# Later stores of x: nine places for the attention output, and the first expert's weights one period later

## The chip, the cores and the metric

The kernel runs on one core of a Trainium2 chip. The metric is device microseconds from the start to the end of one execution, and less is better. The core has TensorE (PE; its weight loads are listed as PEld), VectorE (DVE), ScalarE (ACT), GpSimd (POOL) and SyncE (SP), which here only issues DMAs; 16 DMA engines move the data.

## The reference, cut to what matters

Chunked attention (each head in chunks of 64 tokens, softmax inside a chunk) makes x, and a mixture of experts with one expert per token works on x. Which expert a token goes to depends on the logits of x, and, where the local gate says so, on the token before it.

```python
B, H, S, D = q.shape            # 8, 8, 576, 64
scores = scale * np.matmul(q_c, k_c.transpose(0, 1, 2, 4, 3))   # chunks of 64
attn = np.exp(scores - np.max(scores, axis=-1, keepdims=True))
attn = attn / (np.sum(attn, axis=-1, keepdims=True) + 1e-09)
x = np.matmul(attn, v_c) ...    # then (8, 576, 512)

logits = np.einsum('bsd,de->bse', x, w_gate)                    # 8 experts
local_gate = 1.0 / (1.0 + np.exp(-np.einsum('bsd,de->bse', x, w_local).squeeze(-1)))
...
        for s in range(S):
            fresh_e = int(np.argmax(logits[b, s]))
            if s == 0 or local_gate[b, s] < 0.5:
                e = fresh_e
            else:
                e = prev_e if prev_e >= 0 else fresh_e
            prev_e = e
            ls = logits[b, s] - logits[b, s].max()
            p = np.exp(ls)
            p /= p.sum() + 1e-09
            h = np.maximum(x[b, s] @ w1[e], 0.0)                # w1: 512 x 1024 each
            out[b, s] = p[e] * (h @ w2[e])                      # w2: 1024 x 512 each
```

## The kernel before

The 4608 tokens are 18 tiles of 256, numbered 0 to 17. The attention runs as a pipeline of periods written out by hand: period i makes the scores of tile i+1 (`sc`), transposes of its probabilities later on, the values of tile i-1 (`o`, then x by the divide of line 267 into `xs`), the transposes and the router logits of tile i-2 (`xs` read, its last columns filled by line 316), the transposes of q and k of tile i+2, and on GpSimd the copies that pair the heads of tile i+3. Periods 1 to 15 are a loop; what comes before and after is written as two long lists, "start" and "drain".

In a period TensorE's order is: scores, transposes of `xs`, the first half of the values, transposes of q, router, transposes of k, the second half of the values, router transposes, transposes of the probabilities. The two halves share one tile of PSUM, `o`, so that the second half waits until VectorE has written the first into `xs`.

Loads and stores of this part are issued by SyncE, in the order that the framework settles on; at most eight of its DMAs are under way, since each waits for the one eight before it. In period i they are q and k of tile i+5 (three buffers each), v of tile i+2 (three buffers, the third of them in the memory of the raw half of w2 until tile 12, then two), and the store of x of tile i-2 to `x_d` in DRAM (line 318), right after its logits are there. x has three places (`xs`, three buffers), so tile i's x goes to the place of tile i-3 and its first write waits for the landing of that store. The first expert's w1 (four quarters, `raw1`) is loaded at the ends of periods 9 to 12, its w2 at the ends of 13 and 14, and w1 is split into a high part (ScalarE, line 102) and a low part (GpSimd, line 103) at the ends of periods 11 to 14.

```python
xss[i] = pa2.tile([P, 2, XR], F32, name="xs", bufs=3)              # a_va, the values of tile i
...
nc.sync.dma_start(x_d[256 * i:256 * i + 256, :].rearrange("(c p) n -> p c n", p=P), xs)   # red, line 318
...
        if 9 <= i < 13:                                            # end of period i
            load_w1(0, i - 9)
        if i in (13, 14):
            for c in range(2 * i - 26, 2 * i - 24):
                load_w2(0, c)
        if 11 <= i < 15:
            for col in (slice(0, 512), slice(512, F)):
                split(w1h[i - 11][:, col], w1l[i - 11][:, col], raw1[i - 11][:, col], nc.gpsimd)
```

After the periods the tokens are sorted by expert, gathered in tiles of 128 from `x_d` by indirect DMAs on GpSimd, and put through w1 (line 646) and w2 (line 660). Three tiles of the first expert are gathered early, from the first 2304 tokens (tiles 0 to 8), so that their matmuls fill the drain. The experts take the time from about 166 us to the end.

Of the kernel before, what the change touches and what calls it, by code (L numbers as in the profile page):

```python
# [8 lines left out]
F32 = mybir.dt.float32  # L9
F32R = mybir.dt.float32r  # L10
# [12 lines left out]
C = H * D  # L23
N = B * S
P = 128
NT = N // P
NS = N // 256
XR = C + E + 1
# [30 lines left out]
    "t1": "AAAA",  # L59
    "t2": "AVAA",  # L60
    "steady": "lq s*8 s h0 tx*8 s va*4 va tq*8 ra*2 h1 tq*8 pr*4 va*4 lv va ra*2 h2 tp*8 s h3 ",
    "hooks": [47, 47, 49, 49, 51, 51, 53, 54, 55, 55, 57, 58, 58, 59, 59, 61, 62, 62],
}

# [2 lines left out]
def tile_attention_then_moe(ctx: ExitStack, tc, q, k_in, v, wg, wl, w1, w2, out):  # L67
    nc = tc.nc

    cpool = ctx.enter_context(tc.tile_pool(name="cpool", bufs=1))  # L70
    wpool = ctx.enter_context(tc.tile_pool(name="wpool", bufs=1))
    dpool = ctx.enter_context(tc.tile_pool(name="dpool", bufs=1, space=DRAM))

    x_d = dpool.tile([N, XR], F32, name="x_d")
# [10 lines left out]

    w1h = [wpool.tile([P, F], F32R, name=f"w1h{c}") for c in range(4)]
    w1l = [wpool.tile([P, F], F32R, name=f"w1l{c}") for c in range(4)]
    w2h = [wpool.tile([P, 2, C], F32R, name=f"w2h{c}") for c in range(4)]
    w2l = [wpool.tile([P, 2, C], F32R, name=f"w2l{c}") for c in range(4)]
    pair1 = [wpool.tile([P, 2, F], F32, name=f"raw1_{g}") for g in range(2)]  # L90
    pair2 = [wpool.tile([P, 4, C], F32, name=f"raw2_{g}") for g in range(2)]
    raw1 = [pair1[c // 2][:, c % 2] for c in range(4)]
    raw2 = [pair2[c // 2][:, c % 2 * 2:c % 2 * 2 + 2] for c in range(4)]

    def load_w1(e, c):
        nc.sync.dma_start(raw1[c], w1[e, P * c:P * c + P, :])
# [4 lines left out]
    def split(hi, lo, raw, lo_eng=None):  # L101
        nc.scalar.copy(hi, raw)  # L102
        (lo_eng or nc.vector).tensor_tensor(lo, raw, hi.bitcast(F32), ALU.subtract)  # L103
# [5 lines left out]
    pa2 = ctx.enter_context(tc.tile_pool(name="pa2", bufs=2, side="right"))  # L109
# [8 lines left out]
    vbuf = [pa1.tile([P, 2, H, DV], F32, name=f"v{i}") for i in range(2)]  # L118
    vbuf.append(pair2[1].rearrange("p a c -> p (a c)")[:, 0:2 * H * DV].rearrange("p (c h d) -> p c h d", c=2, h=H))
    V3 = 12  # L120

    def cut(i):
        n = -256 * i % S
# [166 lines left out]
    def router(i, xT, xs, fine=False):  # L290
        lg = ps_l.tile([P, 2, 256], F32, name="lg")
        lT = pa2.tile([P, 2, 256], F32, name="lT", bufs=1)

        def mm():
            for c in range(4):
                nc.tensor.matmul(lg[32 * c:32 * c + 32, 0], wg9[:, c], xT[:, c], start=True, stop=True)  # L296
            if not fine:
                cp()

        def cp():  # L300
            nc.vector.tensor_copy(lT[:, 0], lg[:, 0])
            nc.vector.tensor_copy(lT[:, 1].rearrange("p (c a q) -> p a c q", a=2, c=2),
                                  lg[:, 0].rearrange("p (a c q) -> p a c q", a=2, c=2))

        def tr():
            for cc in range(2):
                nc.tensor.transpose(lg[:, 1, P * cc:P * cc + P], lT[:, 0, P * cc:P * cc + P], ident)
            for cc in range(2):
                nc.tensor.transpose(lg[:, 0, P * cc:P * cc + P], lT[:, 1, P * cc:P * cc + P], ident)
            if not fine:  # L310
                red()

        def red():
            Lt = L[:, 2 * i:2 * i + 2, :]
            for n, dst in ((0, xs[:, :, C:XR]), (1, Lt)):
                nc.vector.tensor_reduce(
                    dst, lg[:, n].rearrange("p (t c e) -> p t e c", t=2, c=4)[:, :, 0:9, :], AX.X, ALU.add)
            nc.sync.dma_start(x_d[256 * i:256 * i + 256, :].rearrange("(c p) n -> p c n", p=P), xs)

        return [mm, cp, tr, red] if fine else [mm, tr]  # L320

    def ok(i):
        return 0 <= i < NS
# [123 lines left out]
    qk, hd, vts, qkT, prs, pTs, xss, xTs = ({} for _ in range(8))  # L447
# [15 lines left out]
        return p_transposes(prs.pop(i), pTs[i], fine)  # L463

    def a_va(i, fine=False):
        xss[i] = pa2.tile([P, 2, XR], F32, name="xs", bufs=3)
        return values(pTs.pop(i), vts.pop(i), xss[i], fine)

    def a_tx(i, fine=False):
# [359 lines left out]
    for i in range(1, NS - 2):  # L829
        qs4 = dict(s=lambda: a_sa(i + 1), tp=lambda: a_tp(i), va=lambda: a_va(i - 1, True), tq=lambda: a_tq(i + 2))  # L830
        opt = dict(lq=load(qk, load_qk, i + 5) if ok(i + 5) else None,
                   lv=(lambda: [lambda: load_vs(i)]),
                   pr=(lambda: a_pair(i + 3)) if ok(i + 3) else None, tx=(lambda: a_tx(i - 2)) if i >= 2 else None, ra=(lambda: a_ra(i - 2, True)) if i >= 2 else None)
        for h in range(4):
            opt[f"h{h}"] = (lambda h=h: [lambda: run(hooks[i, h])]) if (i, h) in hooks else None
        toks = [t for t in PAR["steady"].split() if opt.get(t.split("*")[0], 1) is not None]
        play(" ".join(toks), qs4 | {k: v for k, v in opt.items() if v is not None})
        if 9 <= i < 13:
            load_w1(0, i - 9)
        if i in (13, 14):  # L840
            for c in range(2 * i - 26, 2 * i - 24):
                load_w2(0, c)
        if 11 <= i < 15:
            for col in (slice(0, 512), slice(512, F)):
                split(w1h[i - 11][:, col], w1l[i - 11][:, col], raw1[i - 11][:, col], nc.gpsimd)

    def w2_split(c):
        return [lambda: nc.scalar.copy(w2h[c], raw2[c]),
# [4 lines left out]
    n = NS - 1  # L853
# [265 lines left out]
```

## Time and profile before

| what | value |
|---|---|
| time, median of 3 runs | 673.91 us (673.85 to 678.2) |
| the profiled execution: time, span | 675.2 us, 673.4 us |
| PE, DVE, ACT, POOL busy | 633.6, 362.6, 267.5, 150.8 us |
| bytes moved | 98.23 MB, mean 146 GB/s |
| share of 16 DMA engines in the first nine slices of 16.8 us | 0.9 and more in each |

The span is the time from the first to the last instruction in the profile. Rows of stretches give, after the bounds and the length, the busy time and the count of instructions of PE, PEld, DVE, ACT and POOL, then TensorE's granted clock (1.00 is its full level of 2.4 GHz, 0.50 the lower one of 1.2 GHz), the busy share of the DMA engines (packets that overlap can take it above 1) and GB/s. In rows of waits and of timelines the arrow points to what ended the wait. A line of scores, `sc`, is the first work of a period on TensorE: period 4 begins at 47.07 us, period 13 at 122.06 us.

### The profile page before, as it was taken

The page shows a single profiled execution, that of the slowest core. Times are in us where ns is not written, and L with a number is a line of the kernel's source. Part 1 is how long each engine was busy: PE and PEld are TensorE (multiplying, and loading weights), DVE is VectorE, ACT ScalarE, POOL GpSimd, SP SyncE. Part 2 cuts the span into 40 slices and gives each one's busy share as a digit, 9 for nine tenths or more (in the row PEclk, how much of TensorE's full clock was granted, in tenths as well). Part 3 has the DMA queues.
Part 4 walks back from the last instruction along what each step waited for, and adds up shares of the span by engine and source line. Part 5 has one row for each costly group of instructions (what it writes and reads, how often), then busy time and mean ns, then how long its engine had stood idle before and what let it go on. Part 6 is the DMA issues. An engine that isn't in the chain of part 4 may idle for free.

```text
span 673.4 us, 16385 instructions
## 1 busy us (share of the span) xinstructions
PE 633.6 (94%) x5684; PEld 503.2 (75%) x5684; DVE 362.6 (54%) x936; ACT 267.5 (40%) x439; POOL 150.8 (22%) x214
## 2 busy tenths in 40 slices
PE   5899989888999999999999999999999999999993
PEld 4677777666777887778888877788877888768872
DVE  2656667686787376663232466643467422564230
ACT  4657667656322235442122343422454222442220
POOL 5323224472022111211121121221122211212101
PEclk9989999998999999999999999999999999999998
DMA  9999999995614114545111153551148511244101
GB/s 230 249 229 258 236 264 280 301 282 164 236 37 143 33 49 174 177 160 177 35 64 34 33 191 145 191 172 44 38 171 292 176 38 34 66 158 167 48 19 37
DMA packets 102829, 98.23 MB, mean 146 GB/s; under 512 B 42388, under 2 KB 79252, under 8 KB 102676
## 3 DMA queue, kind: packets, MB, share of 16 engines
q1 hardware_dynamic: 88644, 61.01, 32.7%
q0 software_dynamic: 6640, 20.65, 9.2%
q10 hardware_dynamic: 7392, 14.68, 6.2%
q8 instruction: 77, 1.26, 0.8%
q14 instruction: 76, 0.62, 0.3%
HBM read 77.28 MB, written 20.35 MB: 145 GB/s over the span
## 4 chain that ended last, share of the span: by engine, by line
PE 39%; issue 26%; DMA 23%; DVE 5%; SPq 3%; POOL 2%; POOLq 1%; ACT 0%; DVEq 0%
DMA out<-ysb,sidx 14%; PE y L660 12%; PE h L646 12%; DMA x_d<-xs 7%; PE tr L174 4%; SPq L135 3%; PE o L253 2%; PE tr L740 2%; DVE xs L267 2%; PE tr L725 1%; PE y L667 1%; POOL rh L441 1%; DMA qt<-in_q 1%; PE h L654 1%; PE lg L296 1%
## 5 line engine op out<-in xcount | busy, mean ns | idle before, releaser
L660 PE MATMUL y<-w2h,hp 128*128 128x512 f32 x560 | 185.8, 401 | 1.0 <-ACTq L954 1.0
L646 PE MATMUL h<-w1h,xp 128*128 128x512 f32 x560 | 161.6, 398 | 0.0
L775 POOL DMA_INDIRECT out<-ysb,sidx x41 | 41.9, 1021 | 369.9 <-DVE ysb L772 284.3
L660 PEld LDWEIGHTS y<-w2h,hp 128*128 128x128 f32 x560 | 105.2, 188 | 24.8 <-ACTq L954 1.2
L646 PEld LDWEIGHTS h<-w1h,xp 128*128 128x128 f32 x560 | 102.1, 188 | 20.1 <-issue 0.2
L660 PE MATMUL y<-w2l,hp 128*128 128x512 f32 x280 | 110.7, 395 | 0.1
L646 PE MATMUL h<-w1l,xp 128*128 128x512 f32 x280 | 87.3, 393 | 0.4 <-DVEq L954 0.4
L713 ACT CAST hp<-tr 128x512 fp32r<-128x512 f32 x64 | 34.9, 589 | 119.5 <-PE tr L740 116.8
L772 DVE TENSOR_SCALAR ysb<-y,ppr 128x512 f32<-128x512 f32 x35 | 26.3, 750 | 87.4 <-PE y L660 68.1
L646 PEld LDWEIGHTS h<-w1l,xp 128*128 128x128 f32 x280 | 52.5, 188 | 12.4 <-DVEq L954 0.9
L660 PEld LDWEIGHTS y<-w2l,hp 128*128 128x128 f32 x280 | 52.7, 188 | 11.5 <-DVEq L954 0.6
L699 ACT ACTIVATE hsb<-h 128x1024 f32<-128x1024 f32 x35 | 35.9, 1026 | 60.2 <-PE h L646 57.6
L714 DVE TENSOR_TENSOR xp<-tr,xp 128x512 fp32r<-128x512 f32 x32 | 22.1, 690 | 58.9 <-ACTq L954 56.2
L714 DVE TENSOR_TENSOR hp<-tr,hp 128x512 fp32r<-128x512 f32 x64 | 41.6, 685 | 15.5 <-ACT hp L713 13.7
L632 ACT ACTIVATE pex<-pex 128x8 f32<-128x8 f32 x41 | 8.6, 209 | 102.4 <-DVE pex L631 89.1
L613 POOL DMA_INDIRECT xg<-x_d,gidx x39 | 41.4, 1063 | 14.1 <-issue 10.1
L740 PEld LDWEIGHTS tr<-ident,hsb 128*128 128x128 f32 x274 | 31.9, 140 | 9.0 <-ACTq L954 3.3
L740 PE MATMUL tr<-ident,hsb 128*128 128x128 f32 x274 | 37.3, 274 | 1.4 <-DVEq L954 1.4
L103 DVE TENSOR_TENSOR w1l<-raw,w1h 128x1024 fp32r<-128x1024 f32 x28 | 33.0, 1222 | 8.3 <-ACT w1h L102 8.3
L103 DVE TENSOR_TENSOR w2l<-raw,w2h 128x1024 fp32r<-128x1024 f32 x28 | 32.4, 1220 | 3.9 <-ACT w2h L102 3.9
L166 POOL COPY qr<-qt 128x512 f32<-128x512 f32 x34 | 19.9, 613 | 65.3 <-PE tr L174 44.0
L267 DVE TENSOR_TENSOR xs<-o,rs 128x512 f32<-128x512 f32 x36 | 24.9, 693 | 14.5 <-DMA x_d<-xs 13.6
(210 smaller groups left out, 851.5 us busy)
## 6 DMA issues: line engine op xcount, KB each, us to landing
raw<-in_moe_w SPq DMA_DIRECT2D x14, 1024.0 KB
raw<-in_moe_w ACTq DMA_DIRECT2D x14, 1024.0 KB, 6.4
x_d<-xs SPq DMA_DIRECT2D x18, 521.0 KB, 6.0
raw<-in_moe_w SPq DMA_DIRECT2D x16, 512.0 KB
v<-in_v SPq DMA_DIRECT2D x26, 256.0 KB, 7.0
qt<-in_q SPq DMA_DIRECT2D x11, 512.0 KB, 6.5
kt<-in_k SPq DMA_DIRECT2D x11, 512.0 KB, 7.6
qt<-in_q SPq DMA_DIRECT2D x16, 128.0 KB, 3.8
```

Of the source, the lines that this page charges most:

```text
L103: (lo_eng or nc.vector).tensor_tensor(lo, raw, hi.bitcast(F32), ALU.subtract)
L174: nc.tensor.transpose(box["ps"][:, n], src_of(n), ident)
L267: nc.vector.tensor_tensor(xs[:, :, 256 * j:256 * j + 256].rearrange("p c (h d) -> p c h d", d=D), ov[:, :, :, 0:D], rs.unsqueeze(3).to_bro ...
L613: nc.gpsimd.indirect_dma_start(out=dst, out_offset=None, in_=src, in_offset=bass.IndirectOffsetOnAxis(ap=gidx[t].bitcast(U32), axis=0))
L646: nc.tensor.matmul(hs[:, j], xs[a][:, c], W1[w][c][:, 512 * j:512 * j + 512], start=(c == 0 and n == 0), stop=(c == 3 and n == 2))
L660: nc.tensor.matmul(y, hx[f // 4][a][:, f % 4], W2[w][c][:, f % 2, :], start=(f == 0 and n == 0), stop=(f == 7 and n == 2))
L699: nc.scalar.activation(hsb, hs.rearrange("p j f -> p (j f)"), AF.Relu)
L713: nc.scalar.copy(p[:, 0], ps)
L714: V.tensor_tensor(p[:, 1], ps, p[:, 0].bitcast(F32), ALU.subtract)
L740: nc.tensor.transpose(ps[:, n], hsb[:, at + P * n:at + P * n + P], ident)
L772: either(kind and kind[1], lambda: V.tensor_scalar(ysb, y, pr, None, ALU.mult), lambda: y_part(ysb, y, pr))
L775: nc.gpsimd.indirect_dma_start(out=out, out_offset=bass.IndirectOffsetOnAxis(ap=sidx[t].bitcast(U32), axis=0), in_=ysb, in_offset=None, bo ...
```

## The change

The store of x leaves the router. Of tiles 0 to 13 it is issued at the end of a later period, by a table: tile 0 at the end of period 6 (before: in period 2), and so on to tile 5 at the end of period 11; tiles 6 and 7 after period 12, 8 and 9 after 13, 10 and 11 after 14, 12 and 13 after 15. Tiles 14 to 17 are stored at once, as before. x of tiles 0 to 5 and 9 to 11 is kept in six places (`ring`) that lie in the memory of the split w2 (`x_w2h`, `x_w2l`), which is written only in the drain; x of tiles 6 to 8 and 12 to 17 uses the three buffers `xs`. So tiles 9, 10 and 11 follow 0, 1 and 2 in their places, and 12, 13 and 14 follow 6, 7 and 8. The first expert's w1 and w2 are loaded, and w1 split, one period later each.

```diff
+    "stores": {6: (0,), 7: (1,), 8: (2,), 9: (3,), 10: (4,), 11: (5,), 12: (6, 7), 13: (8, 9), 14: (10, 11), 15: (12, 13)},
...
-    w2h = [wpool.tile([P, 2, C], F32R, name=f"w2h{c}") for c in range(4)]
-    w2l = [wpool.tile([P, 2, C], F32R, name=f"w2l{c}") for c in range(4)]
+    w2h, w2l = [], []
+    early = [wpool.tile([P, 8 * C], F32, name=f"x_{tag}", tag=tag) for tag in ("w2h", "w2l")]
...
+    ring = [t[:, 2 * XR * n:2 * XR * n + 2 * XR].rearrange("p (c n) -> p c n", c=2) for t in early for n in range(3)]
+    held = {}
...
-            nc.sync.dma_start(x_d[256 * i:256 * i + 256, :].rearrange("(c p) n -> p c n", p=P), xs)
+            held[i] = xs
+            if i >= 14:
+                store_x(i)
...
+    def store_x(i):
+        nc.sync.dma_start(x_d[256 * i:256 * i + 256, :].rearrange("(c p) n -> p c n", p=P), held.pop(i))
...
-        xss[i] = pa2.tile([P, 2, XR], F32, name="xs", bufs=3)
+        n = i if i < 6 else i - 9 if 9 <= i < 12 else None
+        xss[i] = pa2.tile([P, 2, XR], F32, name="xs", bufs=3) if n is None else ring[n]
...
-        if 9 <= i < 13:
-            load_w1(0, i - 9)
-        if i in (13, 14):
-            for c in range(2 * i - 26, 2 * i - 24):
+        if 10 <= i < 14:
+            load_w1(0, i - 10)
+        for n in PAR["stores"].get(i, ()):
+            store_x(n)
+        if i in (14, 15):
+            for c in range(2 * i - 28, 2 * i - 26):
                 load_w2(0, c)
-        if 11 <= i < 15:
+        if 12 <= i < 16:
             for col in (slice(0, 512), slice(512, F)):
-                split(w1h[i - 11][:, col], w1l[i - 11][:, col], raw1[i - 11][:, col], nc.gpsimd)
+                split(w1h[i - 12][:, col], w1l[i - 12][:, col], raw1[i - 12][:, col], nc.gpsimd)
+
+    for dst, tag in ((w2h, "w2h"), (w2l, "w2l")):
+        t = wpool.tile([P, 4, 2, C], F32R, name=tag, tag=tag)
+        dst += [t[:, c] for c in range(4)]
```

SyncE's queue, before, from the load of v of tile 12 (`v0`) on: `xs_1765`, `xs_1936` and `xs_2100` are x of tiles 8, 9 and 10, `qt_2043` belongs to tile 16 and `qt_2221` to tile 17, and `raw1` takes quarters 1, 2 and 3 of w1.

```order
L149 DMA v0_118<-in_v 128x8x64 x2
L318 DMA x_d_63<-xs_1765 128x2x521
L96 DMA raw1_0_89<-in_moe_w1 128x1024
L135 DMA qt_2043<-in_q 128x8x128
L135 DMA kt_2044<-in_k 128x8x128
L149 DMA v1_119<-in_v 128x8x64 x2
L318 DMA x_d_63<-xs_1936 128x2x521
L96 DMA raw1_1_90<-in_moe_w1 128x1024
L135 DMA qt_2221<-in_q 128x8x128
L135 DMA kt_2222<-in_k 128x8x128
L318 DMA x_d_63<-xs_2100 128x2x521
L96 DMA raw1_1_90<-in_moe_w1 128x1024
```

The same queue, changed, from v of tile 13 (`v1`) on: `x_w2l_82` is x of tile 5, `qt_2198` belongs to tile 17, `xs_1421`, `xs_1586` and `xs_1749` are x of tiles 6, 7 and 8, `v0` is v of tile 14 and `x_w2h_81` x of tiles 9 to 11; `raw1` takes quarters 1, 2 and 3.

```order
L152 DMA v1_113<-in_v 128x8x64 x2
L97 DMA raw1_0_83<-in_moe_w1 128x1024
L328 DMA x_d_63<-x_w2l_82 128x2x521
L138 DMA qt_2198<-in_q 128x8x128
L138 DMA kt_2199<-in_k 128x8x128
L97 DMA raw1_1_84<-in_moe_w1 128x1024
L328 DMA x_d_63<-xs_1421 128x2x521
L328 DMA x_d_63<-xs_1586 128x2x521
L97 DMA raw1_1_84<-in_moe_w1 128x1024
L328 DMA x_d_63<-xs_1749 128x2x521
L152 DMA v0_112<-in_v 128x8x64 x2
L328 DMA x_d_63<-x_w2h_81 128x2x521 x3
```

So the loads of q, k and v stand four stores further ahead at first. From tile 17's q and k on the stores close up, and the place that x of tile 12 needs (that of tile 6; before, that of tile 9) stands behind all 18 tiles of q and k, three quarters of w1 and six other stores; the place of tile 9 stood behind 17 tiles of q and k, two quarters and nine other stores.

GpSimd at the end of period 14 and in 15, before: the pairing of k of tile 17, the one-hots of the router (`rh`), the low part of w1's last quarter (`w1l3`), and the three early gathers of x into `raw1`.

```order
L166 COPY kr_2691<-kt_2222 128x4x128 x2
L441 TENSOR_SCALAR rh_121<-iota_m_131,rq_122 128x128 x12
L103 TENSOR_TENSOR w1l3_80<-raw1_1_90,w1h3_76 128x512 x2
L613 DMA raw1_0_89<-x_d_63,gidx0_2952 128x521 x2
L613 DMA raw1_1_90<-x_d_63,gidx0_2952 128x521
```

The same, changed.

```order
L169 COPY kr_2668<-kt_2199 128x4x128 x2
L449 TENSOR_SCALAR rh_115<-iota_m_125,rq_116 128x128 x12
L104 TENSOR_TENSOR w1l2_79<-raw1_1_84,w1h2_75 128x512 x2
L622 DMA raw1_0_83<-x_d_63,gidx0_2929 128x521 x2
L622 DMA raw1_1_84<-x_d_63,gidx0_2929 128x521
L104 TENSOR_TENSOR w1l3_80<-raw1_1_84,w1h3_76 128x512 x2
```

The last quarter's low part now stands behind the gathers; the quarter before it has its old place.

## Rows read from the trace of the kernel before

**Rows 1.** Stretches: us, busy us by engine, PE clock, DMA share, GB/s

```profile
47.07:78.73 31.66, 30.08 (x689) 24.64 (x688) 21.84 (x57) 21.69 (x37) 9.37 (x16) 1.00 1.02 250
78.73:112.48 33.75, 30.40 (x689) 24.83 (x688) 21.86 (x57) 21.74 (x37) 9.37 (x16) 1.00 1.08 269
...
122.06:131.97 9.91, 7.88 (x177) 6.37 (x175) 6.62 (x23) 6.91 (x14) 4.74 (x6) 1.00 1.11 283
131.97:139.82 7.85, 7.84 (x176) 6.42 (x175) 5.71 (x15) 5.58 (x10) 4.84 (x6) 1.00 1.07 295
139.82:151.85 12.03, 9.41 (x192) 7.37 (x191) 11.54 (x41) 6.46 (x12) 9.02 (x14) 0.90 1.05 282
...
165.85:420.00 254.15, 252.76 (x1509) 199.63 (x1509) 143.54 (x398) 85.90 (x142) 43.16 (x46) 1.00 0.33 113
```

**Rows 2.** Waits, 47 to 152 us: us in total, times, longest

```profile
DVE xs L267 <- DMA x_d<-xs: 13.6, 9, 2.5
...
PE o L253 <- DVE xs L267: 9.1, 9, 2.3
```

**Rows 3.** Timeline of TensorE: start us, us, what, [idle before <- releaser]

```profile
47.07 1.16 PE L204 MATMUL sc<-kT,qT 64*64 64x64 f32 x64
...
52.43 0.70 PE L253 MATMUL o<-v,pT 64*64 64x65 f32 x32
...
54.51 1.16 PE L204 MATMUL sc<-kT,qT 64*64 64x64 f32 x64
...
122.06 1.16 PE L204 MATMUL sc<-kT,qT 64*64 64x64 f32 x64
...
129.06 0.70 PE L253 MATMUL o<-v,pT 64*64 64x65 f32 x32 [1.45 <-DVE xs L267]
...
131.97 1.16 PE L204 MATMUL sc<-kT,qT 64*64 64x64 f32 x64
...
141.93 0.70 PE L253 MATMUL o<-v,pT 64*64 64x65 f32 x32
...
175.87 0.71 PE L646 MATMUL h<-w1h,xp 128*128 128x512 f32 x2
```

**Rows 4.** The chain that ended last, 104 to 135 us: start us, us, what

```profile
121.99 6.22 DMA x_d<-xs
...
128.31 0.70 DVE xs L267
```

**Rows 5.** Timeline of SyncE's queue: start us, us, DMA issued

```profile
129.82 2.28 SPq L149 DMA_DIRECT2D v<-in_v  x2
```

**Rows 6.** DMA packets, queue and issues: count, KB each, us to landing

```profile
DMA packets 102829, 98.23 MB, mean 146 GB/s; under 512 B 42388, under 2 KB 79252, under 8 KB 102676
...
q1 hardware_dynamic: 88644, 61.01, 32.7%
...
x_d<-xs SPq DMA_DIRECT2D x18, 521.0 KB, 6.0
raw<-in_moe_w SPq DMA_DIRECT2D x16, 512.0 KB
v<-in_v SPq DMA_DIRECT2D x26, 256.0 KB, 7.0
qt<-in_q SPq DMA_DIRECT2D x11, 512.0 KB, 6.5
kt<-in_k SPq DMA_DIRECT2D x11, 512.0 KB, 7.6
```

**Rows 7.** Two short stretches with a clock change, columns as in Rows 1

```profile
145.00:149.50 4.50, 2.02 (x52) 1.45 (x51) 4.33 (x14) 1.12 (x2) 4.50 (x9) 1.00 0.93 296
149.50:152.90 3.40, 3.26 (x60) 2.84 (x61) 3.26 (x9) 1.53 (x3) 2.83 (x3) 0.50 1.08 292
```

**Rows 8.** Timeline of ScalarE near the last attention period

```profile
141.41 1.14 ACT L102 CAST w1h<-raw 128x512 fp32r<-128x512 f32 x2
...
154.30 0.59 ACT L164 COPY pT<-tr 128x512 f32<-128x512 f32 x1 [0.80 <-PE sc L204]
```

## The prediction

> **What bounds the kernel now.** I read the stretches first. From 165.85 to 420 us TensorE is busy 252.76 of 254.15 us [rows 1], so what happens before 166 us is passed on to the end one for one, and what the change touches lies there. In the attention periods it is otherwise: from 47.07 to 78.73 us TensorE works 30.08 of 31.66 us, and in period 13 (122.06 to 131.97) only 7.88 of 9.91, while the DMA engines' share is 1.02 to 1.11 throughout [rows 1]. The waits say where the idle time sits: VectorE's write of x waited 13.6 us, nine times, for a landing of the store that frees its place, and TensorE's second half of the values waited 9.1 us behind it [rows 2]. A period without such a wait takes 54.51 - 47.07 = 7.44 us [rows 3]. Last I read the chain: tile 9's store goes out at 121.99 us, takes 6.22 us, and x of tile 12 is written at 128.31, right at its landing [rows 4]; TensorE's second half follows at 129.06, after 1.45 us idle [rows 3].
>
> The question is then whether a store is late because it is *issued* late, or because the one queue of SyncE is *full*. I count what stood ahead of it. By the sizes in the list of issues a tile of q and k is 1024 KB, of v 512, of x 521, a quarter of w1 512 [rows 6]. Up to tile 9's store the queue held 17 tiles of q and k, 14 of v, 10 of x and 2 quarters: 17408 + 7168 + 5210 + 1024 = 30810 KB, 31.55 MB. They had landed by 128.2 us, a mean of 246 GB/s, and the stretches show 250 to 295 [rows 1]. So that store landed when the queue had worked through what stood ahead of it. It is the queue that bounds this part.
>
> The Trainium skill speaks against this reading. Its page "DMA: Bandwidth & Descriptors", section Bandwidth, has 425 GB/s for a single transfer of 16 MB, issued by GpSimd, with one core at work; at that rate 31.55 MB would pass in an estimated 74 us and the queue would be empty most of the time. No row here comes near it: 295 GB/s is the most at a share of 1.07 [rows 1], and 79252 of 102829 packets are under 2 KB [rows 6]. By the rate of that page of the Trainium skill the time would be that of the faster rival below.
>
> **The change part by part.**
>
> *The waits of periods 5 to 12 go.* Tiles 0 to 8 each have a fresh place, and 9 to 11 follow 0 to 2, stored three periods before. The loads of q, k and v move ahead by up to four stores, so they aren't late either. TensorE then runs 7.44 us a period and begins period 13 at 47.07 + 9 x 7.44 = 114.0 us, 8 us sooner than the 122.06 of now [rows 3].
>
> *A long wait in period 13 takes their place.* x of tile 12 goes where tile 6 was, and tile 6 is stored after period 12. Ahead of it and with it the queue has all 18 tiles of q and k, 14 of v, 7 of x and 3 quarters of w1: 18432 + 7168 + 3647 + 1536 = 30783 KB. That is 27 KB less than what stood up to tile 9's store before. The two stores end the same wait of the same tile, and the same bytes stand ahead of them. TensorE, ready for its second half at 114.0 + 5.36 = 119.4 us (52.43 - 47.07 [rows 3]), would wait until about 129.8: some 10 us at one place, in place of many short waits, and the 8 us are given back.
>
> How exactly the landing moves has bounds. By bytes it is 27 KB sooner, 0.1 us. By packets it is later: q and k are 79252 - 42388 = 36864 packets in 18 tiles [rows 6], 2048 a tile; a store has 256 rows, a quarter 128; so +2048 + 128 - 3 x 256 = +1408 packets, each 32.7% x 673.4 us / 88644 = 2.48 ns of all engines [rows 6], +3.5 us. And if the engines were kept at a share of 1.11 [rows 1] where they had some 1.05 over the 75 us before 122, the landing could be 4 us sooner. So -4 to +3.5 us. I take +0.8, between bytes and packets and nearer to bytes: the stretch with most small packets moved 250 GB/s, those with more stores and weights 269 to 295 [rows 1], so packets count, but not alone.
>
> *TensorE's clock.* In 145.0 to 149.5 us TensorE worked 2.02 of 4.5 us; in the next 3.4 us the granted clock was 0.50, the lower level of 1.2 GHz, with TensorE busy for 3.26 us [rows 7]. Half of that, 1.6 us, is what the lower level cost. A wait of 10 us is longer than that one, and behind it TensorE is the bound: in period 14 it is busy 7.84 of 7.85 us [rows 1]. The lower clock may fall wholly into the wait (0) or twice onto work (3.3). I take one stretch, +1.6 us. The Trainium skill's page "TensorE: Matmul & The Clock Gate", section Part 1: The HAM clock gate, says that the gate sets the clock by how busy the engine has been; the trace agrees, with 0.50 behind the 2.5 us idle.
>
> *The first expert's weights.* The loads stay ahead of what needs them: w1 is first multiplied at about 166 us and its last quarter at 175.87 [rows 3], 24 us after the last period. GpSimd's low part of that quarter now stands behind the early gathers and is done long before; without that cover it would cost its own few us. On ScalarE the two casts of the last quarter, 1.14 us together, move from 141.41 us to the end of period 15, ahead of a copy at 154.30 that has 0.80 us idle before it [rows 8]: 1.14 - 0.80 = 0.3 us, bounds 0 and 0.6. I take +0.3.
>
> *Other queues.* v of tile 14 now stands behind tile 8's store, and it waits, as before, until tile 12's values are read. It was issued by 129.82 + 2.28 = 132.1 us [rows 5], lands some 7.0 us later [rows 6] and is read at 141.93 [rows 3]: 2.8 us of cover, which moves with period 13; nothing, or as much as it is late beyond that. From tile 11's store on both queues hold the same in the same order, so v of 15 and the stores of 12 and later land as before. The early gathers need tiles 0 to 8, which land near 134 us, before period 15 begins (139.82 [rows 1]). The cast that first writes the split w2 now waits for the stores of tiles 9 to 11; these stand ahead of w2's own load, which it waits for anyway: nothing.
>
> **Sum.** +0.8 + 1.6 + 0.3 = +2.7 us. The profiled execution took 675.2 us, 1.8 more than its span and 1.3 more than the median; its successor would take 677.9, and the median goes from 673.9 to **676.6 us**. With the bounds (-4 to +7.4) this case alone spans 670 to 681.
>
> **The rivals.**
>
> *Faster: the queue isn't full.* If the queue is mostly empty and a store lands right behind its issue, the waits vanish and period 14 begins at 47.07 + 10 x 7.44 = 121.5 us, not at 131.97 [rows 3]: -10.5 us, 663.4 us. For it: SyncE's stores wait for data that is just made, which would no longer hold up the queue. Against: tile 6's store would have to land by 118 us, 267 GB/s from the start where 246 was had.
>
> *Slower: bunched stores and one long pause.* If packets set the pace, tile 6's store lands 3.5 us later, at 131.7 us; the pause grows to 12 us and the lower clock falls twice onto work, 3.3 us; with 0.6 on ScalarE that is +7.4, 681.3 us. It decides from a landing at about 131 us on; beyond, v of tile 14 loses its cover too, and each us adds one.
>
> *It changes nothing at all.* The order of the queue shows that the stores do move, but if the wait simply returns at the same landing and the clock falls into it, the time is 674.
>
> **How the numbers follow.** The forecast has 0.65, the faster rival 0.17, the slower 0.10, no change 0.08. One per cent, 6.7 us, is about what a measurement here tells from no change. Faster by over 1% (under 667.2) is the faster rival, 0.16; slower by over 1% (over 680.6) the slower one, 0.10; within it 0.74. The range reaches from 667, into the faster rival's shortfalls, to 681.
>
> **What would show it.** No wait of VectorE's write of x for a store from 47 us to period 12, periods of 7.4 us, period 13 beginning near 114; then one wait of 8 to 11 us that ends with tile 6's landing at 128 to 130 us, and a stretch of clock 0.50 behind it; the first matmul of w1 2 to 4 us later than now. The prediction is wrong if that landing comes before 124 us, if TensorE already waits for q, k or v in periods 8 to 12, or if the drain waits for stores.

## The result, and the profile after

The changed kernel took 678.57 us (median of 22 runs, 675.78 to 681.98), the kernel before 673.82 us (22 runs, 669.75 to 679.25). The ratio is 1.0075, with a 95% interval of 1.0054 to 1.0096: some 4.7 us slower, inside the 1% band. The profiled execution of the changed kernel took 675.78 us, the shortest of its 22, with a span of 674.0 us; a second profile of the same kernel, taken with the experiments, has a span of 678.9 us. I read both, since they differ in just the place that matters.

The waits from 47 to 152 us of the changed kernel, first profile: us in total, times, longest.

```profile
PE o L256 <- DVE xs L270: 13.9, 2, 12.1
DVE xs L270 <- DMA x_d<-xs: 12.9, 1, 12.9
```

Against [rows 2] the nine waits of VectorE's write of x have become one, of nearly their sum: 12.9 us for 13.6. TensorE's timeline shows where it lies.

```profile
113.58 1.16 PE L207 MATMUL sc<-kT,qT 64*64 64x64 f32 x64
...
131.23 1.15 PE L256 MATMUL o<-v,pT 64*64 64x65 f32 x32 [12.10 <-DVE xs L270]
...
135.28 1.48 PE L207 MATMUL sc<-kT,qT 64*64 64x64 f32 x64
...
155.18 1.74 PE L207 MATMUL sc<-kT,qT 64*64 64x64 f32 x64
...
165.87 0.70 PE L655 MATMUL h<-w1h,xp 128*128 128x512 f32 x2
```

Period 13 begins 8.5 us sooner than in [rows 3] (113.58 for 122.06), and its second half of the values waits 12.1 us, so that period 14 begins 3.3 us later than before (135.28 for 131.97). The stretches of [rows 1] read so now (columns as there):

```profile
47.07:78.73 31.66, 31.66 (x735) 26.13 (x736) 23.65 (x61) 23.13 (x39) 9.40 (x16) 1.00 0.98 233
78.73:112.48 33.75, 32.98 (x742) 26.91 (x743) 25.79 (x71) 24.09 (x41) 11.49 (x20) 1.00 1.06 260
...
122.06:131.97 9.91, 0.74 (x28) 0.74 (x32) 1.35 (x3) 0.00 (x0) 0.00 (x0) 0.52 1.08 349
131.97:139.82 7.85, 7.85 (x149) 6.58 (x141) 4.96 (x15) 4.86 (x9) 2.52 (x3) 0.74 0.91 249
...
165.85:420.00 254.15, 251.98 (x1505) 199.38 (x1505) 143.24 (x397) 86.11 (x142) 42.57 (x45) 1.00 0.34 116
```

Up to 112 us TensorE hardly pauses. From 122 to 132 the compute engines all but stand still (TensorE works 0.74 us, VectorE 1.35) while the DMA engines move 349 GB/s, and the clock is lower in that stretch and the next (0.52, 0.74). Behind 165.85 TensorE is busy throughout, as before.

The chain of the first profile has tile 6's store ahead of VectorE's write (start us, us, what):

```profile
122.51 7.88 DMA x_d<-xs
...
130.49 0.70 DVE xs L270
```

And the chain of the second profile at the same place:

```profile
128.55 6.95 DMA x_d<-xs
...
135.59 0.70 DVE xs L270
```

The store goes out at 122.51 us and lands 7.88 us later; in the second profile it goes out 6.0 us later and lands after 6.95. SyncE's timeline tells what went out ahead of it. A row is the time that SyncE spends on an issue, not the transfer. In the first profile:

```profile
115.34 1.61 SPq L97 DMA_DIRECT2D raw<-in_moe_w  x1
...
118.03 1.70 SPq L138 DMA_DIRECT2D kt<-in_k  x1
119.78 2.63 SPq L97 DMA_DIRECT2D raw<-in_moe_w  x1
122.51 1.95 SPq L328 DMA_DIRECT2D x_d<-xs  x2
...
132.41 1.00 SPq L152 DMA_DIRECT2D v<-in_v  x2
```

In the second:

```profile
118.73 3.20 SPq L97 DMA_DIRECT2D raw<-in_moe_w  x1
...
123.02 1.83 SPq L138 DMA_DIRECT2D kt<-in_k  x1
124.90 3.56 SPq L97 DMA_DIRECT2D raw<-in_moe_w  x1
128.55 0.90 SPq L328 DMA_DIRECT2D x_d<-xs  x2
```

SyncE doesn't pause here: from the first of these rows to the store, each issue begins within 0.1 us of the end of the one before. Where it does wait for a buffer, the pause stands ahead of the row: v of tile 14, at 132.41 us, begins 6.2 us after the last issue ended. So the store was held by the issues ahead of it in SyncE's order, which take long: the two quarters of w1 (line 97) took 1.61 and 2.63 us, in the second profile 3.20 and 3.56, where the first two quarters of the kernel before took 0.46 each. Why an issue takes longer no row tells.

Both chains put a copy of GpSimd (line 169) ahead of the load of k (line 138), as if that load had waited for a buffer. It hadn't. It is the load of tile 17's k, which takes the buffer of tile 14, and GpSimd had copied tile 14's k by 104.67 us, in the second profile by 107.56. In the kernel before the same load went out ahead of the copies of tile 16's k, which the chains name (SyncE's and GpSimd's timelines):

```profile
125.80 0.53 SPq L135 DMA_DIRECT2D kt<-in_k  x1
```

```profile
127.80 1.16 POOL L166 COPY kr<-kt 128x512 f32<-128x512 f32 x2
```

How much had been moved by the landing is nearly the same in all three profiles: 32.44 MB in the kernel before (tile 9's store, 128.22 us), 32.84 MB in the first profile (tile 6's, 130.39 us) and 32.68 MB in the second (135.50 us). The mean pace up to there was 253, 252 and 241 GB/s. The second profile is slow early; its first two stretches are to be read against 250 and 269 GB/s in [rows 1] and 233 and 260 in the first profile:

```profile
47.07:78.73 31.66, 31.66 (x764) 26.29 (x754) 22.74 (x58) 23.56 (x40) 9.37 (x16) 1.00 1.01 230
78.73:112.48 33.75, 31.97 (x737) 26.40 (x736) 24.88 (x67) 23.09 (x40) 9.44 (x17) 1.00 0.96 230
```

TensorE's timeline of the second profile carries the delay on:

```profile
136.34 1.15 PE L256 MATMUL o<-v,pT 64*64 64x65 f32 x32 [14.61 <-DVE xs L270]
...
139.99 1.16 PE L207 MATMUL sc<-kT,qT 64*64 64x64 f32 x64
...
158.67 1.16 PE L207 MATMUL sc<-kT,qT 64*64 64x64 f32 x64
...
169.85 0.70 PE L655 MATMUL h<-w1h,xp 128*128 128x512 f32 x2
```

So period 14 is 8.0 us later than before; the span grows by 5.5 us (678.9 for 673.4).

### The profile page after: what moved, and what is told of

Read it like the earlier page. It is cut to its first block, busy times and chain, and to the rows that moved or that the text cites. A ratio compares the mean times of both kernels' runs of the same rounds, so it can differ in the third digit from the quotient of the medians.

```text
span 674.0 us, 16390 instructions
## 1 busy us (share of the span) xinstructions
PE 631.3 (94%) x5684; PEld 502.7 (75%) x5684; DVE 363.1 (54%) x936; ACT 267.8 (40%) x439; POOL 149.8 (22%) x214
## 3 DMA queue, kind: packets, MB, share of 16 engines
q1 hardware_dynamic: 88644, 61.01, 32.8%
## 4 chain that ended last, share of the span: by engine, by line
PE 43%; issue 26%; DMA 19%; DVE 5%; SPq 4%; POOL 1%; POOLq 1%; ACT 0%; DVEq 0%; ACTq 0%
DMA out<-ysb,sidx 14%; PE y L669 12%; PE h L655 12%; PE tr L177 7%; SPq L138 3%; PE o L256 2%; DMA x_d<-xs 2%; PE sc L207 2%; PE tr L749 2%; PE lg L299 1%; PE tr L734 1%; PE y L676 1%; DMA qt<-in_q 1%; PE h L663 1%; PE lg L310 1%
## 5 line engine op out<-in xcount | busy, mean ns | idle before, releaser
L256 PE MATMUL o<-v,pT 64*64 64x65 f32 x896 | 20.8, 228 | 14.6 <-DVE xs L270 14.2
```

The lines of the kernel that those rows point to most:

```text
L256: nc.tensor.matmul(o[64 * cp:64 * cp + 64, cc, DV * h:DV * h + D + 1], pT[64 * cc:64 * cc + 64, 4 * j + h, 64 * cp:64 * cp + 64], vt[64 * ...
```

## The experiments

The ratios are to the kernel before on the same chip. The table puts the landmarks of all profiles side by side, in us: the scores that open period 4, those that open period 14, the last scores, the first matmul of w1, the span, and the median from issue to landing of the early gathers. The landmarks of a row are those of one execution; the ratio rests on 6 to 30 runs of each kernel.

| kernel | ratio (95%) | period 4 | period 14 | last scores | first w1 | span | gathers |
|---|---|---|---|---|---|---|---|
| before | | 47.07 | 131.97 | 151.85 | 165.85 | 673.4 | 4.3 |
| changed, 1st | 1.0075 (1.0054 to 1.0096) | 45.12 | 135.28 | 155.18 | 165.87 | 674.0 | 3.6 |
| changed, 2nd | 1.008 (1.005 to 1.011) | 46.82 | 139.99 | 158.67 | 169.85 | 678.9 | 3.7 |
| weights back | 1.0159 (1.013 to 1.0188) | 45.77 | 141.75 | 161.33 | 177.60 | 685.3 | 8.4 |
| weights later alone | 0.998 (0.9963 to 0.9997) | 44.72 | 131.16 | 150.80 | 163.33 | 671.3 | 5.2 |
| stores at once | 0.998 (0.9953 to 1.0007) | 48.51 | 128.27 | 148.92 | 165.18 | 673.1 | 6.7 |
| tiles 12, 13 elsewhere | 0.996 (0.9943 to 0.9977) | 46.00 | 122.85 | 146.22 | 157.46 | 668.8 | 7.0 |
| same, weights back | 0.9963 (0.9939 to 0.9986) | 47.06 | 125.21 | 149.47 | 162.18 | 671.0 | 6.4 |
| tile 6 a period sooner | 1.009 (1.0056 to 1.0124) | 45.02 | 134.06 | 153.63 | 170.37 | 678.8 | 8.4 |
| tiles 6, 7, 8 at once | 1.0041 (1.0019 to 1.0062) | 45.09 | 124.17 | 146.13 | 166.07 | 674.1 | 6.4 |
| TensorE kept busy | 1.0109 (1.0077 to 1.0141) | 47.34 | 139.84 | 159.74 | 169.88 | 681.4 | 3.5 |
| stores from ScalarE | 0.9966 (0.9944 to 0.9988) | 44.85 | 127.63 | 147.15 | 159.34 | 668.7 | 4.2 |
| before, stores from ScalarE | 1.0058 (1.0039 to 1.0077) | 48.96 | 130.29 | 150.05 | 166.01 | 675.2 | 6.8 |
| 12, 13 elsewhere, from ScalarE | 0.9978 (0.9959 to 0.9996) | 48.03 | 125.73 | 149.80 | 161.88 | 672.4 | 5.2 |

**The weights in their old periods.** The changed kernel with the second part undone.

```diff
-        if 10 <= i < 14:
-            load_w1(0, i - 10)
+        if 9 <= i < 13:
+            load_w1(0, i - 9)
...
-        if i in (14, 15):
+        if i in (13, 14):
...
-        if 12 <= i < 16:
+        if 11 <= i < 15:
```

> The changed kernel with the first expert's weights loaded and split in their old periods. Theory A (the queue: what counts is what stands in SyncE's queue ahead of the store that frees tile 12's place): one more quarter of w1, 512 KB, stands ahead of tile 6's store, about 2 us at 250 GB/s; TensorE's one long wait grows from 12.1 to about 14 us and the time goes to about 1.010 of the kernel before. Theory B (the clock: the price is the lower clock behind the long wait): the same wait with the same clock, no change against the changed kernel, 1.0075. Theory C (the weights that come later cost the time): it gets faster, 1.003 or less.

It took 687.16 us, 1.0159. The one wait is 12.98 us on TensorE and ends at 138.12, 6.9 us later than in the first profile of the changed kernel and 1.8 later than in the second. The first theory has the direction, but neither its wait of 14 us nor its 1.010: period 13 itself begins at 119.59, 6.0 us later than in the first profile. The earlier weights stand ahead of tile 6's store; the drain, too, is longer, 16.3 us (177.60 - 161.33), with gathers that take 8.4 us. So inside the change its second part takes away some of the loss of the first.

**Tiles 12 and 13 in early places.** Tile 12 goes where tile 3 was and tile 13 where tile 4 was, so that nobody waits for tile 6's store.

```diff
-        n = i if i < 6 else i - 9 if 9 <= i < 12 else None
+        n = i if i < 6 else i - 9 if 9 <= i < 14 else None
```

> The changed kernel with x of tiles 12 and 13 in the places of tiles 3 and 4, which are stored by period 10. Theory A: the long wait in period 13 is gone, period 14 begins at about 121.5 us; the next thing late is v of tile 14, which the same queue brings at about 135 us, so period 15 waits for it some 5 us; time 0.990 to 0.994 of the kernel before. Theory B: no long pause, no lower clock in period 13 or 14; 2 to 3 us of the gain. Rival (the bytes of the whole queue set the end of the attention, whatever the places): the wait only moves to v and the time is 1.000 or more.

672.38 us, 0.996: faster than both kernels, though not by as much as the 0.990 to 0.994 expected, and without the wait for v of tile 14. TensorE's timeline has no wait for a place in period 13:

```profile
114.46 1.16 PE L207 MATMUL sc<-kT,qT 64*64 64x64 f32 x64
...
122.85 1.16 PE L207 MATMUL sc<-kT,qT 64*64 64x64 f32 x64
```

The one wait is thus shown to be the loss of the change: 12 to 17 us sooner into period 14, and 0.996 for 1.0075. It also shows what the waits were worth. Without any, period 14 begins 9.1 us sooner than in the kernel before, but the span is only 4.6 us shorter and the median 2.4.

**Tile 6 stored one period sooner.**

```diff
-... 11: (5,), 12: (6, 7), 13: ...
+... 11: (5, 6), 12: (7,), 13: ...
```

> The changed kernel with tile 6 stored after period 11 and not 12; in the queue its store then stands ahead of tile 17's q and k and of the third quarter of w1, 1536 KB or about 6 us. Theory A: the wait in period 13 ends at about 124.5 us and is 5 to 6 us long, tile 13's place (that of tile 7) is late by at most 2 us, period 14 begins at about 127 to 129 us; time 0.996 to 1.000. Theory B: a wait of 5 us is still followed by a stretch of the lower clock, so half or less of the gain: 1.002 to 1.004. Rival (the whole queue): 1.0075, unchanged.

681.26 us, 1.009, where 0.996 to 1.000 was expected. Two timelines, of SyncE's queue and then of TensorE:

```profile
121.16 2.52 SPq L328 DMA_DIRECT2D x_d<-xs  x1
```

```profile
130.20 1.15 PE L256 MATMUL o<-v,pT 64*64 64x65 f32 x32 [9.57 <-DVE xs L270]
```

A place one period sooner in the program is an issue only 1.4 us sooner than in the first profile (121.16 for 122.51), though 7.4 sooner than in the second; the wait ends at 130.20 us, and period 14 begins at 134.06. The time doesn't fall even so: between the last scores and the first matmul of w1 pass 16.7 us, where the changed kernel has 10.7 and 11.2, and the early gathers take 8.4 us. Of this, 3.89 us are one pause of TensorE (160.74 to 164.62) right ahead of the transposes that read the first gather; the profile names nothing that ended it, so that the gather's part is likely, but not shown.

**TensorE kept busy in the wait.** 64 transposes that nobody reads, in period 13 ahead of the second half of the values.

```diff
-... h1 tq*8 pr*4 va*4 ...
+... h1 tq*8 dm pr*4 va*4 ...
...
+    def busy():
+        ps = trp()
+        for n in range(64):
+            nc.tensor.transpose(ps[:, P * (n % 4):P * (n % 4) + P], ident, ident)
```

> The changed kernel with 64 transposes of the identity (about 8 us of TensorE's work, not used) in period 13, between the transposes of k and the second half of the values, where TensorE waits 12.1 us. Theory B: the granted clock stays at 1.00 in the wait and behind it, period 14 begins at about 133.5 and not 135.3 us, and the time goes down by 1.5 to 3 us, to 1.003 to 1.005 of the kernel before. Theory A alone (the landing decides, the clock costs little): the wait ends at the same 131 us and the time stays at 1.0075. If the extra work itself costs, 1.009 or more.

TensorE's timeline in period 13:

```profile
122.59 7.21 PE L841 MATMUL tr<-ident 128*128 128x128 f32 x64 [0.33 <-ACT kT L167]
135.79 1.14 PE L256 MATMUL o<-v,pT 64*64 64x65 f32 x32 [5.99 <-DVE xs L270]
```

681.71 us, 1.0109. The landing came at 135 us, as in the second profile, so that 5.99 us of wait were left behind the 7.21 us of transposes, and the half clock still fell on the values that follow (1.14 us for 32 matmuls). The lower clock could not be taken away in this way; its price isn't told apart here. Nor is a cost of the extra work: the interval overlaps that of the changed kernel (1.005 to 1.011).

**The second part alone.** The kernel before with the first expert's weights one period later: the edit of the first experiment, the other way round, on the kernel before.

> The kernel before with the second part of the change alone: the first expert's weights come and are split one period later, stores and places of x as before. Theory A (the place: what counts is when the store on which a value of x waits has landed, and everything on SP's queue ahead of it delays it): half a MB less stands in the queue from period 9 on, so the waits of periods 9 to 12 shrink by about 2 us in all, and the values of period 13 begin 1 to 3 us sooner than at 129.1; ratio to the kernel before 0.995 to 0.999. Theory D (what comes a period later bunches ahead of the early gathers): the median from issue to landing of the early gathers' rows rises from 4.3 us to 7 or more and the stretch from the last scores to the first matmul of w1 from 14.0 to 16 us; ratio 1.002 to 1.006.

674.00 us, 0.998, inside the first theory's range; the interval of the ratio just leaves out 1. But what that theory named didn't come: the waits for places are 14.2 us in ten (13.6 in nine before), and from period 4 to period 14 the kernel takes 86.4 us, where before it took 84.9. That period 14 begins 0.8 us sooner (131.16) comes from a start that was 2.4 us sooner, so the number was met by luck. The gathers took 5.2 us and the drain 12.5 (14.0 before), so bunching ahead of the gathers isn't what the later weights bring.

**Nine places, stores at once.**

```diff
             held[i] = xs
-            if i >= 14:
-                store_x(i)
+            store_x(i)
...
-        for n in PAR["stores"].get(i, ()):
-            store_x(n)
```

> The changed kernel with its six more places for x, but every tile stored at once, as in the kernel before, instead of four periods later; weights as in the changed kernel. Tile 12 takes the place of tile 6, whose store is then issued six periods before its place is wanted. Theory A: no value of x waits at all up to the end of attention, period 13 begins near 113.6 and period 14 near 121 to 123, as in the run with tiles 12 and 13 in other places; ratio to the kernel before 0.993 to 0.998. The rival (the queue's bytes set the time whatever the places): the 1.06 MB stores stand among the loads again, and TensorE waits for q, k or v in periods 5 to 13, 8 us or more in sum; ratio 0.999 to 1.004.

675.35 us, 0.998, on the edge between the two expectations. The waits for places went, as the first theory says: until 152 us no write of x waits for a store. But period 13 begins at 118.86 and period 14 at 128.27, not near 113.6 and 121 to 123; 3.4 us of that are there at period 4 already (48.51 for 45.12). And two other waits take their place, which TensorE's timeline names:

```profile
141.39 0.68 PE L256 MATMUL o<-v,pT 64*64 64x65 f32 x28 [1.17 <-DMA v<-in_v]
...
159.49 1.09 PE L615 MATMUL tr<-ident,raw 128*128 128x128 f32 x4 [3.90 <-DMA raw<-x_d,gidx]
```

The load of v is late, and then the early gathers. Putting the stores off is therefore what costs in the change: with the same places and the same weights, but stores at once, the kernel is about 1% faster (0.998 for 1.008).

**The changed kernel again.**

> The changed kernel itself once more, for a second profile: its first profiled execution took 675.78 us, the shortest of its 22. Theory A: the wait for tile 6's place ends at 129 to 132 again, and period 14 begins at 134 to 137. If theory D holds, the stretch from the last scores to the first matmul of w1, 10.7 us in the first profile, is 14 to 17 us in an execution of 678 to 681 us; if it is near 11 us again, the time is in the start-up or in the experts.

680.69 us, 1.008, and the second profile shown above. The drain is 11.2 us and not 14 to 17, so the theory of bunched transfers ahead of the gathers falls for the change itself; what grew is the wait in period 13, beyond what I had written for it (its end at 136.3, not 129 to 132; period 14 at 140.0, not 134 to 137).

**Early places for 12 and 13, weights in the old periods.** The two edits of the first two experiments together.

> The changed kernel with tiles 12 and 13 in early places, as in the run that took 0.996 of the kernel before, and with the weights loaded and split in the old periods. It tells what the weights' later period does when no value of x waits for a place. Theory A: with no place to wait for, the half MB that stands ahead delays nobody; ratio 0.993 to 0.998, no wait for a place, first matmul of w1 at 155 to 160. The rival (the weights delay q, k and v themselves): TensorE waits for loads in periods 12 to 15, 2 to 6 us; ratio 1.000 to 1.006.

673.21 us, 0.9963, as the first theory has it (but the first matmul of w1 came at 162.18, later than its 155 to 160), next to the 0.996 with later weights. Where no write waits for a place, the weights' period makes no difference that can be measured; in the changed kernel it makes 0.8%.

**Stores issued by ScalarE.** In the changed kernel, and nothing else moved:

```diff
-        nc.sync.dma_start(x_d[256 * i:256 * i + 256, :]...
+        nc.scalar.dma_start(x_d[256 * i:256 * i + 256, :]...
```

> The changed kernel with all stores of x issued by ScalarE, on its own DMA queue, in the same places of the program; places, order and weights unchanged. Theory A (SP's queue is served in order, and tile 6's store waits behind what is ahead of it there: issue at 122.5, landing 7.9 us later): on a queue of its own it is issued at 120 to 123 and lands in 3 to 5 us, the wait of period 13 shrinks from 12 to 15 us to 3 to 6 us, period 14 begins at 126 to 130; ratio to the kernel before 0.992 to 1.000. The rival (the 16 engines' bytes set the landing, whichever queue holds them): landing at 129 to 136 as before, ratio 1.003 to 1.009.

673.63 us, 0.9966. Timelines of ScalarE and of TensorE:

```profile
114.55 0.45 ACTq L328 DMA_DIRECT2D x_d<-xs  x1
...
115.04 0.48 ACTq L328 DMA_DIRECT2D x_d<-xs  x1
```

```profile
123.59 1.14 PE L256 MATMUL o<-v,pT 64*64 64x65 f32 x32 [3.48 <-DVE xs L270]
...
127.63 1.99 PE L207 MATMUL sc<-kT,qT 64*64 64x64 f32 x64
```

The wait shrank to 3.48 us, as expected, but not for the reason that I gave. I had the store issued at 120 to 123 us and landing in 3 to 5. It was issued at 114.55, 8 and 14 us sooner than in the two profiles of the changed kernel, and VectorE's write came at 122.84, 8.3 us later: the transfer was no quicker than from SyncE's queue (7.88 and 6.95 us). What a queue of its own removed is the place behind the loads that SyncE still had to issue: the quarter of w1 that stood ahead of the store went out there only at 123.48 us. The Trainium skill's page "DMA: Bandwidth & Descriptors", section Issuing engines are not separate DMA queues, says that issuing from several engines saves only the issuing time, since all transfers share the same 16 engines. The trace agrees on the transfer, 8.3 us for 7.88; but when the store was issued is what counted here.

**The kernel before with its stores from ScalarE.** The same edit on the kernel before.

> The kernel before with one line changed: its stores of x are issued by ScalarE, on its own DMA queue, right where SP issued them. Theory A: the stores land 2 to 4 us after their issue and not 6.0 (median), so the 13.6 us in which values of x wait for a place in periods 5 to 12 shrink below 5 us; ScalarE waits about 1 us a period for the reduction ahead of each store; ratio 0.988 to 0.997. The rival (what the stores gain the loads lose, the engines being busy throughout): the waits go to q, k and v, ratio 0.998 to 1.003, or above where ScalarE's held casts are late.

679.66 us, 1.0058: the waits for places up to period 12 are gone, and from period 4 to the last scores the kernel takes 101.1 us (150.05 - 48.96) where before it took 104.8. Yet it is slower. Period 4 begins 1.9 us later, and the early gathers, at 6.8 us, hold TensorE in the drain, as its timeline shows:

```profile
159.67 1.09 PE L607 MATMUL tr<-ident,raw 128*128 128x128 f32 x4 [3.42 <-DMA raw<-x_d,gidx]
```

So both expectations missed: the ratio is over the first theory's range and over the rival's 1.003. The rival comes nearer, in that what the stores gained was lost elsewhere, but not on the place: the pause named is for the gathers, not for q, k or v. The later start, and 1.6 us that come behind the first matmul of w1, aren't explained.

**Early places and stores from ScalarE together.**

> The kernel of the run that took 0.996 (tiles 12 and 13 in early places), with the stores of x issued by ScalarE on its own queue. Theory A: no value of x waits for a place there already, so there is nothing for the stores to gain; ratio 0.993 to 0.998. If SP's issue time is what holds the loads (the rival), SP is freed of 18 issues and the periods from 13 on run closer to 7.4 us: ratio 0.985 to 0.993.

674.20 us, 0.9978: nothing gained over 0.996, as the first theory has it.

**Tiles 6, 7 and 8 stored at once.** Places and weights as in the changed kernel.

```diff
-... 11: (5,), 12: (6, 7), 13: (8, 9), 14: ...
+... 11: (5,), 13: (9,), 14: ...
...
-            if i >= 14:
+            if i >= 14 or i in (6, 7, 8):
```

> The changed kernel with its places as they are, but tiles 6, 7 and 8, whose places tiles 12, 13 and 14 take, are stored at once in periods 8 to 10; the other stores stay put off and the weights as changed. Theory A (the long wait is for tile 6's store, because that store was put off): its landing then lies 20 us or more ahead of its need, no value of x waits in period 13, period 14 begins at 121 to 126 where the two profiles of the changed kernel have 135.3 and 140.0, and the ratio to the kernel before is 0.993 to 0.998, that of the kernels with other places or another queue. The rival (half of the loss is the weights' later period, the clock or the moved casts, which stay): ratio 1.001 to 1.005.

676.16 us, 1.0041. In period 13 the theory is borne out: no wait for a place, and period 14 begins at 124.17, inside 121 to 126. The ratio is in the rival's range, but the profile shows another reason than the rival's. TensorE's timeline, and then the chain:

```profile
124.17 1.16 PE L207 MATMUL sc<-kT,qT 64*64 64x64 f32 x64
...
158.58 1.14 PE L256 MATMUL o<-v,pT 64*64 64x65 f32 x32 [7.70 <-DVE xs L270]
```

```profile
146.67 10.98 DMA x_d<-xs
...
157.74 0.70 DVE xs L270
```

Tile 15 takes the place of tile 12, and tile 12's store is put off to the end of period 15. With attention 11 to 16 us ahead, that store is now the late one: its issue begins at 146.67 and alone takes SyncE 4.22 us, it lands 10.98 us after that beginning, and TensorE waits 7.70 us. It is the same mechanism, one reuse later; what this wait costs in time was not tried by itself.

## Why the prediction was right, and where not

**The forecast as a whole.** 676.6 us was forecast and 678.57 measured, 0.75% over the kernel before, within the 1% that had 0.74 of the chance, and inside the range. The mechanism was the one named: many short waits become one long one for tile 6's store, and the gain in periods 5 to 12 is given back. Of the signs, no wait up to period 12, the start of period 13 and the clock of 0.50 came; the wait was 12.1 and 14.6 us, not 8 to 11, the landing at 130.4 and 135.5, not 128 to 130, and the first matmul of w1 0.0 and 4.0 us later, not 2 to 4.

**The waits that go: right.** No write of x waits for a store between 47 us and period 13. Most periods are 7.4 us, but from period 4 to period 13 pass 68.5 and 69.4 us for the 67.0 forecast (8.17 and 8.20 us are the longest of the first profile, 9.29 of the second). That period 13 begins at 113.58 and 116.19 for 114.0 is in part luck: period 4 began 1.9 and 0.3 us sooner than in the kernel before.

**The wait in period 13: right in place, mis-sized.** The term of the landing was +0.8 us, within -4 to +3.5. In place of it stand +2.2 in the first profile (130.39 for 128.22) and +7.3 in the second (135.50), beyond the upper bound. "The same bytes stand ahead of them" held: 32.84 and 32.68 MB had been moved by the landing, for 32.44 before. The count of packets held too, 1556 and 1515 more for the +1408 forecast. The step that failed is the one from there to a time: the bounds let the engines' share rise to 1.11, but not fall. Up to the landing it was 1.03 in the first profile and 1.00 in the second, for 1.04 before, and the mean pace 252 and 241 GB/s for 253. At 253 GB/s the second profile's 32.68 MB would have been through at 129.2 us, so 6.3 of its 7.3 us are pace; in the first profile 0.40 MB more are 1.6 of the 2.2 us. Why one execution of the same kernel has the slower pace was not settled.

To its own question, issued late or queue full, the runs add this: SyncE issued without a pause and got to the store late, because the issues ahead took long. Issued by ScalarE, 8 to 14 us sooner and with a transfer as long as ever, the store left TensorE 3.48 us of the wait. So its place in SyncE's order made it late, and the 7 to 8 us behind its issue stayed with either queue.

**The clock: right in kind, mis-sized.** +1.6 us was taken. From the end of the wait to the next scores pass 4.05 us (135.28 - 131.23) and 3.65 us (139.99 - 136.34), where the kernel before took 2.91 (131.97 - 129.06 [rows 3]): +1.1 and +0.7.

**ScalarE's casts and the other queues.** Of the +0.3 us for the casts no sign is to be found: the drain got shorter, not longer. v of tile 14 wasn't late, and the split of w2 waited for no store, as was said. What I had not foreseen is a shorter drain. In the kernel before it took 14.0 us from the last scores to the first matmul of w1, and now 10.7 and 11.2. Most of that is one pause: there TensorE waited 2.64 us for VectorE's write of x, now 0.32 and 0.93. VectorE had started 2.47 us late in that one execution, for no landing of a store, so that I can't put this to the change. The drain of the kernel before was thus long by chance, and part of what makes the forecast come out is luck.

**The sum.** With landing and clock the second profile has 7.3 + 0.7 = 8.0 us at period 14. It gets back 1.2 up to the last scores and 2.8 in the drain, and 1.5 us more come after the first matmul of w1: 8.0 - 1.2 - 2.8 + 1.5 = +5.5 in the span. The forecast took what stands at period 14 to the end one for one; +8.0 so taken would have been over the 1%. The first profile has 2.2 + 1.1 = +3.3, 3.3 back in the drain and 0.6 behind it. The median's +4.7 lies between, nearer to the second.

**The rivals.** The faster one, 663.4 us, priced a kernel without waits. Kernels without the long wait exist in four of the experiments, and the best of them has a median of 672.4. Its price was wrong because it let the whole gain at period 14 through to the end: with 122.85 us there, 1.4 from its 121.5, only 4.6 of 9.1 us reached the span. The slower one, 681.3 us, came near by its time, but its cause, the number of packets ahead, doesn't set the landing alone: with 1556 and 1515 more packets the two profiles land 5.1 us apart. Whether packets add to it was not tried. The one of no change, 674, falls: the interval of the ratio (1.0054 to 1.0096) leaves out 1.

**What stays open** is where the gain of a shorter attention goes in each case. Drains of some 16 us and more stand beside gathers that took 6.4 to 8.4 us, and where the profile names a wait of TensorE for those gathers, as with stores at once, that is shown. But gathers of 7.0 and 6.4 us also stand beside drains of 11.2 and 12.7. The start differs too: period 4 begins at 44.7 to 49.0 us, at 45.12 and 46.82 in two executions of the same kernel.

## What to carry to other kernels

A store that is put off holds its place longer, so write down for every place which store frees it and which write takes it next, to the end of the program: the change cleared one set of such pairs and met the next, and so did the kernel with tiles 6, 7 and 8 at once. In a queue that one engine issues in order, a store is as late as the issues ahead of it; count the bytes ahead, and don't take the pace from one execution. Moving the store to another engine's queue gave back what moving it one period in the program did not. A releaser that a profile infers is to be checked against the program: here the chains named a wait for a buffer that had long been free. And where the DMA engines are busy throughout, taking away 13 us of waits was worth 2.4 us of the median at the most here (0.996); in some of the kernels a load or a gather came late next.

## What the runs showed of the hardware that was not expected

A store of 521 KB took 6.22 us from issue to landing in the kernel before, 7.88 and 6.95 in the changed one, 8.3 from ScalarE's queue to VectorE's use, and 10.98 at the end of period 15 with tiles 6 to 8 at once, of which the issue was 4.22; a queue of its own made it no quicker. SyncE's issue of a 512 KB quarter of w1 took 0.46 us in one place and 3.56 in another, without a wait that the profile shows. Two executions of one program moved the same 32.7 to 32.8 MB at 252 and at 241 GB/s. A granted clock of 0.50 stands behind a pause of TensorE of 3.48 us in the kernel with stores from ScalarE (32 matmuls then take 1.14 us for 0.70), and also behind one of 5.99 us with 7.21 us of transposes ahead of it. With tiles 12 and 13 in early places and SyncE's stores, TensorE also stopped for 2.84 us, with the weights back for 3.10 us, in the middle of the scores that open period 15 without any wait that the profile names; the changed kernel has 0.34 and 0.60 us there in its two profiles. What it waits for was not found.
